# Unread float16 products on TensorE in the first eleven attention tiles

## The chip, the cores and the metric

The kernel runs on one core of one Trainium2 chip. The metric is the device time of one execution in microseconds (us); the time of a kernel is the median of its runs. The profile is of one execution. Engines are named as the profile names them: PE is TensorE (PEld its weight loads), DVE VectorE, ACT ScalarE, POOL GpSimd, SP the queue that issues most of the DMAs.

## The reference

Attention with rotary positions over 4 batches of 8 heads, 576 positions and 64 dimensions, then two feed-forward layers over the 2304 tokens of 512 numbers:

```python
q_rot, k_rot = (rotate(q), rotate(k))
scores = scale * np.matmul(q_rot, k_rot.transpose(0, 1, 3, 2))
scores = scores - np.max(scores, axis=-1, keepdims=True)
attn = np.exp(scores)
attn = attn / (np.sum(attn, axis=-1, keepdims=True) + 1e-09)
x = np.matmul(attn, v)                       # then (2304, 512)
h = np.maximum(np.maximum(x @ w1, x @ w2), x @ w3)
y = h @ w_out                                # moe_w_out, 768 wide inside
h = y @ w_in
out = (h * (1.0 / (1.0 + np.exp(-h)))) @ w_out   # moe2, 2048 wide inside
```

The weights arrive as float64 and are brought to pairs of float16 numbers (a high and a low part) inside the kernel.

## The kernel before

Attention goes by pairs of heads, (batch, pair), and within a pair by tiles of 128 query rows: tiles 0 and 1 of all four pairs of a batch first, then tiles 2, 3 and 4 (tile 4 holds the last 64 rows of both heads). In the order of the program the tiles of batch 0 are numbered here 0 to 19, so tiles 0 and 1 are those of the first pair, 2 and 3 of the second, 4 and 5 of the third, 6 and 7 of the fourth, and 8 to 10 the rest of the first pair.

A pair is loaded (`load_qk`), rotated on DVE or POOL (`qk_rope`, L330 to L334), and turned on PE (`qk_turn`: four transposes for k and four for q, L348, one more for the last 64 positions, L354), with copies out of PSUM on DVE and ACT (L350 to L360). A tile then goes through these steps: scores on PE (`tile_scores`, L387 and L390, or L380 and L381 for a tile of 64 rows), the negative row maximum on DVE (L400), the exponential on ACT for each head (`e`, L407), the division on ACT (L416, L419; reciprocal on DVE, L417), nine transposes on PE (`tile_turn`, L448) with copies on ACT (L452) and DVE (L454), and, once two or three tiles of a pair are turned, the product with v (`av`, L463 and L467). The scores have one buffer, `s`, of three banks: the next tile's scores wait until both exponentials have read the last ones.

Beside these tiles the weights of the first layer are prepared (`prep_w1`): twelve loads of 768 KB each into four staging places, each piece converted on ACT (L214, and L218 for the first) or POOL (L216), joined on DVE (L225, L226), measured on ACT (L140), and split on POOL (L160) and DVE (L163). A staging place is loaded anew once DVE's L226 has read it. From tile 8 on the first layer's products (`moe1`, written by `group`, L538, into the two banks `m` of the ring `ps_m`) are mixed into the tiles.

Each engine works off its instructions in the order of the program. That order is not the order in which the code is written: a scheduler with its own timing of the instructions interleaves the engines' work, and `tc.issue_after(x)` keeps an instruction behind x. So a change of one engine's work can change the order on all of them.

Of the kernel before, what the change touches and what calls it, by code (L numbers as in the profile page):

```python
# [7 lines left out]
F32 = mybir.dt.float32  # L8
F16 = mybir.dt.float16
# [8 lines left out]
P = 128  # L18
# [4 lines left out]
def fused_kernel(  # L23
# [22 lines left out]
    nc = tc.nc  # L46
# [28 lines left out]
    ps_m = Ring(ctx, "ps_m", 2, space=PSUM)  # L75
# [8 lines left out]
    ident = const.tile([P, P], F32, name="ident")  # L84
# [67 lines left out]
    def flat(t):  # L152
        return t.rearrange("p a b -> p (a b)")
# [95 lines left out]
    last = {}  # L249
# [59 lines left out]
    def qk_rope(b, hp):  # L309
        t = raw_t[b, hp]  # L310
        w = w_p.tile([P, 18, D], F32, tag="w", name="w")
        if b:
            with tc.issue_after(last["pool"]):
                return rope_steps(t, w, nc.gpsimd, ((0, 6), (6, 12), (12, 18)))
        if hp == 1:
            with tc.issue_after(last["kd"]):
                rope_steps(t, w, nc.vector, ((8, 16), (16, 18)))
            return rope_steps(t, w, nc.gpsimd, ((0, 4), (4, 8)))
        if hp == 0:
            return rope_steps(t, w, nc.vector, ((8, 16), (0, 8), (16, 18)))  # L320
        return rope_steps(t, w, nc.gpsimd, ((0, 6), (6, 12), (12, 18)))
# [15 lines left out]
    def qk_turn(b, hp):  # L337


        t = raw_t.pop((b, hp))  # L340
        T = t_p.tile([P, 576 + 512], F32, tag="T", name="T")
        K, Q = kd[(NP * b + hp) % NK], qd[(NP * b + hp) % NK]
        for i in (1, 0):
            tr = ps_t.tile([P, 512], F32, tag="tr", name="tr")
            for c in range(4):
                behind = tc.issue_after(last["s"]) if b == 0 and hp > 1 else nullcontext()
                with behind:
                    nc.tensor.transpose(tr[:, c * P:(c + 1) * P], flat(t[:, 8 * i + 2 * c:8 * i + 2 * c + 2, :]), ident)  # L348
            if i == 0:
                last["T"] = nc.scalar.activation(out=T[:, 0:512], in_=tr, func=AF.Copy, scale=0.125).ins  # L350
            else:
                nc.vector.tensor_copy(out=T[:, 512:1024], in_=tr)
        tr = ps_t.tile([P, 512], F32, tag="tr", name="tr")
        nc.tensor.transpose(tr[:, 0:P], flat(t[:, 16:18, :]), ident)  # L354
        nc.scalar.activation(out=T[:, 1024:1088], in_=tr[:, 64:128], func=AF.Copy)
        rs = (slice(0, 64), slice(64, 128))
        for r in rs:
            nc.scalar.activation(out=Q[r, r], in_=tr[r, 0:64], func=AF.Copy, scale=0.125)
        for r in rs:
            last["kd"] = nc.vector.tensor_copy(out=K[r, r], in_=tr[r, 64:128]).ins  # L360
        T_t[b, hp] = T, K, Q
# [8 lines left out]
    def both(s, o, step, n):  # L370

        return bass.AP(tensor=s.tensor, offset=s.offset + o, ap=[list(s.ap[0]), [step, 2], [1, n]])
    evacs = [0]

    def tile_scores(key):
        b, hp, t = key
        T, K, Q = T_t[b, hp]
        s = ps_s.tile([P, 1536], F32, tag="s", name="s")
        if t == 4:
            nc.tensor.matmul(s[:, 0:512], Q, T[:, 512:1024], start=True, stop=True)  # L380
            nc.tensor.matmul(s[:, 512:576], Q, T[:, 1024:1088], start=True, stop=True)  # L381
            s_t[key] = s
            return
        n = P
        qs = T[:, t * P:t * P + n]
        kt = T[:, 512:1024]
        nc.tensor.matmul(both(s, 512, 448, 64), qs, K, start=True, stop=True)  # L387
        for g, o in ((0, 0), (1, 1024)):
            r = slice(64 * g, 64 * g + 64)
            last["s"] = nc.tensor.matmul(s[:, o:o + 512], qs[r], kt[r], start=True, stop=True).ins  # L390
        s_t[key] = s

    def heads(key):
# [27 lines left out]
    def tile_turn(key):  # L421
        b, hp, t = key
        n = P
        e = e_t.pop(key)
        r = int(t > 1)
        q0, w = PARTS[r][:2]
        if (b, hp, r) not in pt_t:
            pt_t[b, hp, r] = pt_p.tile([P, 9, w], F32, tag="pt", name="pt")
        pt = pt_t[b, hp, r]
        o = P * t - q0  # L430
        if t == 4:
            tr = ps_t.tile([P, 512], F32, tag="tr", name="tr")
            for c in range(4):
                nc.tensor.transpose(tr[:, c * P:(c + 1) * P], e[:, c * P:(c + 1) * P], ident)
            t4 = tr.rearrange("p (c g q) -> p c g q", c=4, g=2)
            nc.scalar.activation(out=pt[:, 0:4, o:o + 64], in_=t4[:, :, 0], func=AF.Copy)
            nc.vector.tensor_copy(out=pt[:, 5:9, o:o + 64], in_=t4[:, :, 1])
            tr = ps_t.tile([P, 512], F32, tag="tr", name="tr")
            nc.tensor.transpose(tr[:, 0:P], e[:, 448:576], ident)
            nc.tensor.transpose(tr[0:64, P:2 * P], e[:, 512:576], ident)  # L440
            nc.scalar.activation(out=pt[0:64, 4, o:o + 64], in_=tr[0:64, P:P + 64], func=AF.Copy)
            nc.vector.tensor_copy(out=pt[64:128, 4, o:o + 64], in_=tr[64:128, 64:128])
            return
        for j in range(3):
            tr = ps_t.tile([P, 512], F32, tag="tr", name="tr")
            for i in range(3):
                c = 3 * j + i
                nc.tensor.transpose(tr[:, i * n:(i + 1) * n], e[0:n, c * P:(c + 1) * P], ident[0:n, 0:n])  # L448
            to, of = pt[:, 3 * j:3 * j + 3, o:o + n], tr[:, 0:3 * n].rearrange("p (a n) -> p a n", a=3)
            evacs[0] += 1  # L450
            if evacs[0] % 3 == 1 if evacs[0] < 28 else evacs[0] % 3:
                nc.scalar.activation(out=to, in_=of, func=AF.Copy)  # L452
            else:
                nc.vector.tensor_copy(out=to, in_=of)  # L454
# [28 lines left out]
    def at(j, f, *a):  # L483
        events.setdefault(j, []).append((f, a))
# [14 lines left out]
    for b in range(1, B):  # L499
# [3 lines left out]
            at(u - 2, v_max, b, hp)  # L503
        at(u, v_scale, b)

    def attention():

        for j in range(len(tiles) + 4):
            if j < len(tiles):
                tile_scores(tiles[j])  # L510
                tile_max(tiles[j])
            if 1 <= j <= len(tiles):
                tile_norm(tiles[j - 1])
            if 2 <= j <= len(tiles) + 1:
                tile_turn(tiles[j - 2])
            for f, a in events.pop(j, ()):
                f(*a)
            yield


# [616 lines left out]
    for hp in range(NP):  # L1137
        load_v(0, hp)
    last["max"] = qk_rope(*pairs[0]).ins
    qk_turn(*pairs[0])  # L1140
    wprep = prep_w1(stage1)
    for j in sorted(e for e in events if e < 0):
        for f, a in events.pop(j):
# [133 lines left out]
```

## Time and profile before

| | |
|---|---|
| median of 3 runs | 1037.62 us (1037.03 to 1039.41) |
| the profiled execution | 1035.59 us |
| its span, first to last instruction | 1033.9 us |
| granted clock of TensorE, mean over the span | 0.976 |
| busy: PE, PEld | 962.4 us (93%), 717.0 us (69%) |
| busy: DVE, ACT, POOL | 688.3, 616.3, 489.6 us (67%, 60%, 47%) |

Start times in the rows count from the first instruction of the span. A row gives the start, the time that the row covers (of several equal instructions from the start of the first to the end of the last), the engine, the line, the operation and how many. In brackets stands how long the engine was idle before it, and what ended that wait. [...]

### The profile page before, as it was taken

To read this page: it belongs to the slowest core of one execution; us is meant where nothing else is said; L and a number is where in the kernel's file an instruction comes from. 1 tells how busy PE (TensorE), PEld (TensorE's weight loads), DVE (VectorE), ACT (ScalarE), POOL (GpSimd) and SP (SyncE) were. 2 spreads that over 40 slices of the span, in tenths; PEclk is the share of its full clock that TensorE was granted. 3 is DMA by queue.
4 is the path that set the end of the run, shared out by engine and by line. 5 is a ranking of instruction groups with operands and counts; after the bars stand their busy time and mean duration, and the time that the engine had idled before them with its cause. 6 is when DMAs were issued, how large, how long until landed. Compare 5 with 4: busy or idle time off the path is not lost.

```text
span 1033.9 us, 19511 instructions
## 1 busy us (share of the span) xinstructions
PE 962.4 (93%) x7234; PEld 717.0 (69%) x7234; DVE 688.3 (67%) x1295; ACT 616.3 (60%) x1377; POOL 489.6 (47%) x548
## 2 busy tenths in 40 slices
PE   4677998999999999998999999999999999999997
PEld 2343664666666766655756668777888888888887
DVE  6769877765567655687566646645678767867454
ACT  3778676566666575867767754534455644644352
POOL 6735593961127720354223205536258457346164
PEclk9688999999999999999999999999999999999999
DMA  6943132422334510653444415254345244342201
GB/s 152 280 115 101 33 97 75 129 71 62 102 109 110 137 47 27 189 147 118 144 123 139 143 58 168 82 187 145 128 144 168 92 152 125 108 129 93 90 3 41
DMA packets 126062, 117.99 MB, mean 114 GB/s; under 512 B 47376, under 2 KB 109584, under 8 KB 125968
## 3 DMA queue, kind: packets, MB, share of 16 engines
q1 hardware_dynamic: 124464, 116.03, 37.4%
q8 instruction: 57, 0.93, 0.4%
q10 hardware_dynamic: 1504, 0.72, 0.3%
q14 instruction: 37, 0.30, 0.1%
HBM read 90.51 MB, written 26.21 MB: 113 GB/s over the span
## 4 chain that ended last, share of the span: by engine, by line
PE 62%; DVE 9%; ACT 6%; POOL 6%; DMA 6%; issue 3%; SPq 1%; ACTq 0%; DVEq 0%; POOLq 0%
PE m L538 18%; PE xp L467 6%; PE m L946 5%; PE s L390 5%; PE tr L448 5%; PE mb L946 4%; POOL gsum L893 4%; PE mg L538 3%; PE c L1010 3%; PE a L1010 2%; PE b L1010 2%; POOL yr L981 2%; DVE nb L400 1%; PE d L1010 1%; DVE g L898 1%
## 5 line engine op out<-in xcount | busy, mean ns | idle before, releaser
L538 PEld LDWEIGHTS <-w 128*128 128x128 f16 x1632 | 157.3, 98 | 68.8 <-issue 27.8
L538 PE MATMUL m<-x,w 128*128 128x256 f16 (+1 forms) x1336 | 189.7, 288 | 9.9 <-ACT t L554 4.0
L1010 PEld LDWEIGHTS <-g 128*128 128x128 f16 x1485 | 145.7, 98 | 19.9 <-issue 2.3
L946 PEld LDWEIGHTS <-w8s 128*128 128x128 f16 x1344 | 131.4, 98 | 20.3 <-issue 4.8
L400 DVE TENSOR_REDUCE nb<-s 128x2 f32<-128x1152 f32 (+1 forms) x80 | 98.7, 1234 | 49.4 <-PE s L390 39.5
L212 POOL TENSOR_SCALAR z<-z 128x256 uint16<-128x256 uint16 x64 | 56.0, 875 | 159.2 <-DVE z L211 148.4
L407 ACT ACTIVATE e<-s,nb 128x576 f32<-128x576 f32 x144 | 105.1, 735 | 29.0 <-DVE nb L400 24.9
L419 ACT ACTIVATE e<-e,rec 128x576 f32<-128x576 f32 x144 | 104.5, 768 | 17.8 <-DVE rec L417 17.5
L448 PE MATMUL tr<-ident,e 128*128 128x128 f32 x576 | 97.4, 289 | 14.2 <-ACT T L350 6.2
L787 POOL TENSOR_TENSOR z<-z 128x128 f32<-128x128 f32 (+1 forms) x96 | 59.0, 634 | 105.5 <-DMA z<-zwo 38.4
L448 PEld LDWEIGHTS tr<-ident,e 128*128 128x128 f32 x576 | 69.8, 147 | 50.0 <-issue 13.4
L946 PE MATMUL m<-yr,w8s 128*128 128x256 f16 x768 | 90.8, 273 | 3.7 <-DVE t L952 3.7
L452 ACT ACTIVATE pt<-tr 128x384 f32<-128x384 f32 x119 | 56.8, 486 | 47.9 <-PE tr L448 47.7
L467 PE MATMUL xp<-pt,vd 128*64 128x256 f32 (+1 forms) x512 | 84.6, 419 | 0.0
L390 PE MATMUL s<-T 64*128 64x512 f32 x256 | 83.7, 698 | 0.0
L960 POOL TENSOR_TENSOR z<-t 128x256 f32<-128x256 f32 x32 | 28.0, 875 | 95.8 <-DVE t L952 55.9
L946 PE MATMUL mb<-yr,w8s 128*128 128x256 f16 x576 | 69.9, 274 | 2.3 <-ACT yr L158 2.1
L538 PE MATMUL m<-h,wo 128*128 128x256 f16 (+1 forms) x448 | 64.9, 286 | 0.1
L898 DVE SCALAR_TENSOR_TENSOR g<-gsum,sg,g 128x1024 f16<-128x1024 f32 x36 | 49.1, 1373 | 22.1 <-ACT g L897 21.6
L538 PEld LDWEIGHTS <-wo 128*128 128x128 f16 x512 | 49.3, 98 | 16.9 <-issue 4.0
L897 ACT ACTIVATE g<-gsum,sg 128x1024 f16<-128x1024 f32 x36 | 40.7, 1140 | 32.8 <-POOL gsum L893 32.8
L330 POOL TENSOR_TENSOR w<-qk,sin_sb 128x384 f32<-128x384 f32 (+1 forms) x44 | 45.7, 1058 | 30.4 <-DMA qk<-in_q_dram 16.0
(231 smaller groups left out, 1910.8 us busy)
## 6 DMA issues: line engine op xcount, KB each, us to landing
w8s<-w8scr SPq DMA_DIRECT2D x64, 448.0 KB, 4.2
z<-in_moe_w_in_dram SPq DMA_DIRECT2D x32, 256.0 KB, 3.2
z<-in_moe_w_out_dram SPq DMA_DIRECT2D x32, 256.0 KB, 3.3
w<-in_moe_w_dram SPq DMA_DIRECT2D x6, 768.0 KB, 6.0
wo<-in_moe_w_dram SPq DMA_DIRECT2D x6, 768.0 KB, 4.6
qk<-in_q_dram SPq DMA_DIRECT2D x32, 128.0 KB, 3.0
vd<-in_v_dram SPq DMA_DIRECT2D x16, 256.0 KB, 3.0
zwi<-z SPq DMA_DIRECT2D x32, 128.0 KB, 3.1
```

The costliest lines, as they stand in the source:

```text
L390: last["s"] = nc.tensor.matmul(s[:, o:o + 512], qs[r], kt[r], start=True, stop=True).ins
L400: x = nc.vector.tensor_reduce(out=nb[:, 0:m], in_=both(s, 0, 960, 576) if m > 1 else s[:, 0:576], op=ALU.max, axis=AX.X, negate=True)
L407: x = nc.scalar.activation(out=e[:, HK[g]], in_=s[:, SK[g]], func=AF.Exp, bias=nb[:, g:g + 1], accum_out=sm[:, g:g + 1])
L419: nc.scalar.activation(out=e[:, HK[g]], in_=e[:, HK[g]], func=AF.Copy, scale=r[:, g:g + 1])
L448: nc.tensor.transpose(tr[:, i * n:(i + 1) * n], e[0:n, c * P:(c + 1) * P], ident[0:n, 0:n])
L452: nc.scalar.activation(out=to, in_=of, func=AF.Copy)
L467: nc.tensor.matmul(xp[r, 0:n], v4[:, g, c, :], pt[:, c + 5 * g, :], start=False, stop=(c == 3))
L538: nc.tensor.matmul(ps[:, 0:n], l, r, start=(first and i == 0), stop=(not more and i == len(passes) - 1))
L787: nc.gpsimd.tensor_tensor(out=z[:, o], in0=z[:, x], in1=z[:, y], op=op)
L898: nc.vector.scalar_tensor_tensor(out=l, in0=x, scalar=sg_t[jb], in1=h, op0=ALU.mult, op1=ALU.subtract)
L946: nc.tensor.matmul(o, l, r, start=(i == 0), stop=(i == len(passes) - 1))
L1010: x = nc.tensor.matmul(ps, l, r, start=first, stop=last_, skip_group_check=True)
```

## The change

PE gets 200 more products. Each multiplies the identity matrix, its float32 bytes read as float16, with itself: a weight load of 128x128 and a product of 128x256 float16 into a bank `m` that nobody reads. Fifty stand ahead of the first turn. Ten stand behind the first turn (`pe_q`). In each of the first eleven steps of the loop over tiles seven follow the scores of the step's tile (`pe_s`), and from the third step on seven more follow the turn of that step (`pe_t`), nine times. Nothing of the computation is removed. Since the line numbers shift, L448 of before is L449 of the changed kernel, L407 is L408, L400 is L401, L452 is L453; lines up to L354 stay, and the new product is L514.

```diff
-        nc.tensor.transpose(tr[:, 0:P], flat(t[:, 16:18, :]), ident)
+        last["pe_q"] = nc.tensor.transpose(tr[:, 0:P], flat(t[:, 16:18, :]), ident).ins
...
+        last["pe_s"] = last["s"]
...
-                nc.tensor.transpose(tr[:, i * n:(i + 1) * n], e[0:n, c * P:(c + 1) * P], ident[0:n, 0:n])
+                last["pe_t"] = nc.tensor.transpose(tr[:, i * n:(i + 1) * n], e[0:n, c * P:(c + 1) * P], ident[0:n, 0:n]).ins
...
+    idle = ident.bitcast(F16)
+
+    def warm(n, after=None):
+
+        ps = ps_m.tile([P, 512], F32, tag="m", name="m")
+        with tc.issue_after(after) if after else nullcontext():
+            for _ in range(n):
+                nc.tensor.matmul(ps[:, 0:256], idle[:, 0:P], idle, start=True, stop=True)
...
+            if j < 11:
+                warm(7, last["pe_s"])
+                if j > 1:
+                    warm(7, last["pe_t"])
             yield
...
     last["max"] = qk_rope(*pairs[0]).ins
+    warm(50)
     qk_turn(*pairs[0])
+    warm(10, last["pe_q"])
```

The order on PE at the start of the program, before: the turn of the first pair, the scores of tile 0, the turn of the second pair, the scores of tile 1.

```order
L348 MATMUL tr_222<-ident_78,qk_151 128x128 x4
L354 MATMUL tr_228<-ident_78,qk_151 128x128
L387 MATMUL s_299<-kd_0_122,T_215 128x2x64
L390 MATMUL s_299<-T_215 128x512 x2
L348 MATMUL tr_272<-ident_78,qk_160 128x128 x4
L348 MATMUL tr_266<-ident_78,qk_160 128x128 x4
L387 MATMUL s_316<-kd_0_122,T_215 128x2x64
```

The same place in the changed kernel, with one pair of weight load and product for each run of ten, or seven:

```order
L348 MATMUL tr_273<-ident_78,qk_151 128x128 x4
L354 MATMUL tr_279<-ident_78,qk_151 128x128
L514 LDWEIGHTS ident_78
L514 MATMUL m_286<-ident_78 128x256
...
L387 MATMUL s_361<-kd_0_122,T_266 128x2x64
L390 MATMUL s_361<-T_266 128x512 x2
L514 LDWEIGHTS ident_78
L514 MATMUL m_374<-ident_78 128x256
...
L348 MATMUL tr_334<-ident_78,qk_160 128x128 x4
L348 MATMUL tr_328<-ident_78,qk_160 128x128 x4
L354 MATMUL tr_340<-ident_78,qk_160 128x128
L387 MATMUL s_386<-kd_0_122,T_266 128x2x64
```

The ten stand between the first turn and the scores of tile 0, seven behind these scores; the second pair's last transpose (L354) now stands ahead of the scores of tile 1.

The order on ACT from the exponentials of tile 1 to the first of tile 2, before (`e_322` is tile 1, `e_343` tile 2; `w` and `wo` are staging and weights):

```order
L407 ACTIVATE e_322,sm_323<-s_316,nb_320 128x576 x2
L214 ACTIVATE w_0_138<-w_0_295 128x768
L416 ACTIVATE rec_347<-sm_323 128x2
L218 ACTIVATE w_0_295<-w_0_295 128x768
L419 ACTIVATE e_322<-e_322,rec_347 128x576 x2
L214 ACTIVATE w_0_138<-w_1_312 128x768
L140 ACTIVATE junk_394,w1m_136<-w_0_138 128x768
L214 ACTIVATE w_0_138<-wo_0_141 128x768
L350 ACTIVATE T_368<-tr_375 128x512
L407 ACTIVATE e_343,sm_344<-s_337,nb_341 128x576 x2
```

The same stretch of ACT in the changed kernel (`e_392` is tile 1, `e_421` tile 2, `e_496` tile 3):

```order
L408 ACTIVATE e_392,sm_393<-s_386,nb_390 128x576 x2
L417 ACTIVATE rec_425<-sm_393 128x2
L420 ACTIVATE e_392<-e_392,rec_425 128x576 x2
L350 ACTIVATE T_446<-tr_453 128x512
L408 ACTIVATE e_421,sm_422<-s_415,nb_419 128x576
L214 ACTIVATE w_0_138<-w_0_357 128x768
L408 ACTIVATE e_421,sm_422<-s_415,nb_419 128x576
```

The first weight piece (L214) moves from ahead of tile 1's division to between tile 2's two exponentials; L218, two more L214 and the measuring L140 move behind tile 2's exponentials, and stand ahead of those of tile 3.

The order on PE from the scores of tile 5 to those of tile 6, before (`tr_499` is the turn of q of the fourth pair):

```order
L387 MATMUL s_520<-kd_0_124,T_368 128x2x64
L390 MATMUL s_520<-T_368 128x512 x2
L448 MATMUL tr_474<-ident_78,e_343 128x128 x3
L448 MATMUL tr_540<-ident_78,e_402 128x128 x3
L348 MATMUL tr_499<-ident_78,qk_248 128x128 x4
L448 MATMUL tr_572<-ident_78,e_454 128x128 x3
L463 MATMUL xp_587<-pt_463,vd_0_127 128x256
L448 MATMUL tr_535<-ident_78,e_402 128x128 x3
L387 MATMUL s_556<-kd_0_125,T_492 128x2x64
```

The same stretch in the changed kernel (`tr_609` is the same turn of q):

```order
L387 MATMUL s_646<-kd_0_124,T_446 128x2x64
L390 MATMUL s_646<-T_446 128x512 x2
...
L348 MATMUL tr_609<-ident_78,qk_310 128x128 x4
...
L449 MATMUL tr_666<-ident_78,e_496 128x128 x3
L449 MATMUL tr_661<-ident_78,e_496 128x128 x3
L449 MATMUL tr_714<-ident_78,e_564 128x128 x3
L464 MATMUL xp_729<-pt_573,vd_0_127 128x256
L387 MATMUL s_698<-kd_0_125,T_602 128x2x64
```

That turn of q now follows tile 5's scores with only five of the new products between, where it stood behind two groups of transposes; the transposes of tile 2 (`e_343` before) have moved ahead of tile 5's scores. From PE's row 963 of 12062 on (the new products not counted) PE's order is the same as before; on DVE, ACT, POOL and SP the last difference stands likewise in the first fifth to third of their rows.

## Rows read from the trace of the kernel before

**Rows 1.** By stretch: length, busy PE, PEld, DVE, ACT, POOL, then clock, DMA share, GB/s.

```profile
0.00:110.00 110.00, 71.23 (x326) 39.94 (x327) 79.43 (x141) 74.00 (x163) 60.30 (x64) 0.83 0.54 153
80.00:100.00 20.00, 12.90 (x67) 6.66 (x65) 20.00 (x27) 16.03 (x36) 11.16 (x7) 0.91 0.42 131
110.00:1033.90 923.90, 891.14 (x6911) 677.06 (x6908) 608.88 (x1155) 542.34 (x1215) 429.31 (x485) 0.99 0.36 110
```

**Rows 2.** PE in order of time: the same work at either clock.

```profile
46.23 2.08 PE L390 MATMUL s<-T 64*128 64x512 f32 x4
...
52.51 1.13 PE L390 MATMUL s<-T 64*128 64x512 f32 x4
53.57 0.55 PE L448 MATMUL tr<-ident,e 128*128 128x128 f32 x3
...
60.33 1.11 PE L348 MATMUL tr<-ident,qk 128*128 128x128 f32 x4 [2.94 <-DVE pt L454]
61.24 0.85 PE L448 MATMUL tr<-ident,e 128*128 128x128 f32 x3
...
63.94 2.08 PE L390 MATMUL s<-T 64*128 64x512 f32 x4
65.95 0.88 PE L448 MATMUL tr<-ident,e 128*128 128x128 f32 x6
...
100.07 2.84 PE L538 MATMUL m<-x,w 128*128 128x256 f16 x12 [3.02 <-ACT t L554]
...
193.48 0.60 PE L348 MATMUL tr<-ident,qk 128*128 128x128 f32 x4
```

**Rows 3.** ACT in order of time: first exponentials of the tiles, and a weight piece.

```profile
19.13 0.74 ACT L407 ACTIVATE e<-s,nb 128x576 f32<-128x576 f32 x1 [0.41 <-DVE nb L400]
...
24.38 0.73 ACT L407 ACTIVATE e<-s,nb 128x576 f32<-128x576 f32 x1
...
28.88 0.92 ACT L214 ACTIVATE w<-w 128x768 f32<-128x768 f32 x1 [2.96 <-DMA w<-in_moe_w_dram]
...
35.68 0.73 ACT L407 ACTIVATE e<-s,nb 128x576 f32<-128x576 f32 x1
...
42.18 0.74 ACT L407 ACTIVATE e<-s,nb 128x576 f32<-128x576 f32 x1
...
58.21 0.74 ACT L407 ACTIVATE e<-s,nb 128x576 f32<-128x576 f32 x1 [1.00 <-DVE nb L400]
...
67.52 0.74 ACT L407 ACTIVATE e<-s,nb 128x576 f32<-128x576 f32 x1 [2.38 <-DVE nb L400]
...
75.52 0.73 ACT L407 ACTIVATE e<-s,nb 128x576 f32<-128x576 f32 x1
...
101.58 0.75 ACT L407 ACTIVATE e<-s,nb 128x576 f32<-128x576 f32 x1
```

**Rows 4.** The chain of work that ended last, two of its pieces.

```profile
69.72 4.59 DMA w<-in_moe_w_dram
...
137.36 2.73 PE m L538 x24
```

**Rows 5.** POOL in order of time: the identity, and weight pieces of the first loads.

```profile
1.61 0.29 POOL L264 TENSOR_SCALAR_AFFINE_SELECT ident<-ident 128x128 f32<-128x128 f32 x1
...
38.49 4.66 POOL L216 TENSOR_SCALAR wo<-wo 128x768 uint16<-128x768 uint16 x2
```

**Rows 6.** The first turn on PE, and DVE around it, in order of time.

```profile
9.95 1.09 PE L348 MATMUL tr<-ident,qk 128*128 128x128 f32 x4 [9.95 <-DVE qk L334]
...
10.69 0.69 DVE L334 TENSOR_TENSOR qk<-qk,w 128x512 f32<-128x512 f32 x1
...
13.66 0.46 DVE L360 COPY kd<-tr 64x64 f32<-64x64 f32 x2 [1.68 <-ACT qd L358]
...
17.74 1.36 DVE L400 TENSOR_REDUCE nb<-s 128x2 f32<-128x1152 f32 x1
```

More of the change, by code (lines that the diff above doesn't have):

```diff
@@ L380, in tile_scores @@
             nc.tensor.matmul(s[:, 0:512], Q, T[:, 512:1024], start=True, stop=True)
-            nc.tensor.matmul(s[:, 512:576], Q, T[:, 1024:1088], start=True, stop=True)
+            last["pe_s"] = nc.tensor.matmul(s[:, 512:576], Q, T[:, 1024:1088], start=True, stop=True).ins
             s_t[key] = s
@@ L439, in tile_turn @@
             nc.tensor.transpose(tr[:, 0:P], e[:, 448:576], ident)
-            nc.tensor.transpose(tr[0:64, P:2 * P], e[:, 512:576], ident)
+            last["pe_t"] = nc.tensor.transpose(tr[0:64, P:2 * P], e[:, 512:576], ident).ins
             nc.scalar.activation(out=pt[0:64, 4, o:o + 64], in_=tr[0:64, P:P + 64], func=AF.Copy)
```

## The prediction

> **What bounds the kernel now.** I read the page first, then the busy time by stretch, then PE, ACT and DVE in order of time up to 110 us, and last the chain of waits. The page says that PE is busy 93% of the span and that its clock is low only near the start. The stretches say where [rows 1]: from 110 us on PE works 891.1 of 923.9 us at a clock of 0.99, so that part is PE's and no product can be saved there. Up to 110 us PE works 71.2 us, DVE 79.4 and ACT 74.0, and none is full: there the time goes into a loop. Scores wait for the last exponential, the row maximum for the scores, the exponential for the maximum, and weight pieces stand between them on ACT and DVE. In this part the clock is 0.83 in the mean. What the low clock costs is seen on equal work [rows 2]: a tile's scores take 2.08 us against 1.13, three transposes 0.85 against 0.55, four transposes of a turn 1.11 against 0.60. The clock is low where PE had stood idle before, and comes back in a run without a break: after an idle 2.94 us PE works from 60.33 to 65.95, 5.62 us, at the low level, and the transposes from 65.95 on have the high one.
>
> So the change is worth what it brings forward the tiles by, up to about tile 11 (101.58 in rows 3); after that PE is the bound and its order is the old one, so a lead is kept.
>
> **The price of the new products.** They have the form of L538's, 128x256 float16 with a weight load each: 24 take 2.73 us on the chain, 0.114 us each [rows 4]; at the low clock 12 take 2.84, 0.237 each [rows 2]. The identity is ready at 1.61 + 0.29 = 1.90 us [rows 5]. Fifty from there end at 7.6 us if all have the high clock and at 13.8 if all have the low one. By the run above (5.62 us low, then high) I take 24 at the low clock and 26 at the high one: 1.90 + 5.62 + 2.96 = 10.5 us. The first turn started at 9.95, so it starts 0.5 late, but four transposes take 0.60 instead of 1.09. The other 150 cost 17.1 us at the high clock, 35.6 at the low. PE's idle time up to 110 us is 38.8, of which 9.95 lie before the first turn [rows 1, 6]; 28.8 are left, so 150 at the high clock fit beside idle time and 150 at the low one do not. I take nothing for them on the path: seven stand behind scores, while DVE and ACT work for some 3 us on that tile (L400's 1.36, two exponentials at 0.74), and seven behind a turn, whose copies are then due. Without that cover a run of seven costs 0.8 us, or 1.66 at the low clock. They wait for nothing but a bank `m`: where a scale's maximum (L120) used it, one run waits for DVE's reading, and behind it on PE stand only transposes whose divisions on ACT are later still.
>
> **The sum, by the lead at each tile.**
>
> Tile 0: the second turn needs DVE's L334, which ends at 10.69 + 0.69 = 11.38; turned at the high clock from there it ends at 12.0, half a microsecond earlier, and so do the copies to `kd` at 13.66 [rows 6]. The scores gain 0.95 more, but DVE has the second pair's rotation to finish before the row maximum at 17.74, so that is hidden. Lead 0.5.
>
> Tile 1: scores before had the low clock only in part; of 0.95 I take 0.5 (ends 0 and 0.95).
>
> Tiles 2 and 3: here it is the order. Before, ACT stood 2.96 us in front of the first weight piece until its load had landed at 28.88, with tile 1's division and a turn's copy queued behind it; the exponential of tile 2 came at 35.68, 11.3 us after tile 1's [rows 3]. Now these stand ahead of the piece, which meets its load between tile 2's exponentials. Tile 2 thus gains several microseconds, but L218, two L214 and L140 now stand in front of tile 3, and POOL's pieces for the first loads still run to 38.49 + 4.66 = 43.15 [rows 5]. So what is late next is tile 3's exponential. Of the 2.96 I keep 1.8 at tile 3 (ends 0 and 2.96).
>
> Tile 4: its scores had the low clock (2.08 at 46.23) and were followed directly by the maximum: 0.95.
>
> Tile 6: the run from 60.33 lies on the loop; the exponential of tile 6 waited for it, 9.31 us after that of tile 5 [rows 2, 3]. The kinds shown shrink from 1.11 + 0.85 + 2.08 = 4.04 to 2.28 us, a factor of 0.56; 5.62 us become 3.17, a gain of 2.45. The turn of q at its head, which had waited 2.94 for a copy of DVE, now stands right behind tile 5's scores: I take 1.0 of that (ends 0 and 2.94).
>
> Tiles 7 to 11: between 80 and 100 us DVE has no gap at all [rows 1], and tile 7 waits for a weight load of 4.59 us [rows 4] that DVE's L226 behind tile 6's maximum releases. These move with the lead but do not add to it. The twelve products at 100.07 (2.84, at the high clock 1.37) I count as hidden by DVE (ends 0 and 1.47).
>
> Sum: 0.5 + 0.5 + 1.8 + 0.95 + 2.45 + 1.0 = 7.2 us. The profiled execution took 1035.59, so 1028.4; it was 2.03 below the median of 1037.62, so the median becomes **1030.4**. What the changed order does between 110 and about 200 us I take as nothing, with 1.5 either way.
>
> [...]
>
> **Rivals.**
>
> The clock does not hold. Gaps stay in the loop (ACT and DVE are still shared with the weights), and if PE is low again by tile 3, the clock's own terms go (0.5 + 0.5 + 0.95 + 2.45 = 4.4), the 2.8 of the order remains, and seven products at the low clock on the path take 1.66 of it: a gain of 1.1 to 2.8, about 1035.6. For it: a single idle 2.94 us sufficed before 60.33. Against: the runs of seven stand just in such gaps. [...]
>
> The lead is lost to the weights. If DVE, full from 80 to 100 us, and the reloading of four staging places set the pace by themselves, the tiles come early and the first layer's products wait as before: 1037.6. For it: DVE's 20.0 of 20 us. Against: up to 80 us DVE has idle time, and its pieces there are released by the same tiles that come earlier.
>
> The new products get in the way, so that it is slower. On PE they stand in a fixed order ahead of what comes next: eleven in front of tile 5's scores, fourteen in front of a turn at tile 7. With 63 of the 150 on the path (63 x 0.114 = 7.2) the gain is gone; with 90 it is 3 us slower, 1040.6. Against: PE's 28.8 us of idle time.
>
> More than forecast: with the upper ends of tiles 1, 2, 6 and the late products the sum is 0.5 + 0.95 + 2.96 + 0.95 + 2.45 + 2.94 + 1.47 = 12.2, or 1025.4.
>
> **How the numbers follow.** A measurement of this kernel can tell about 0.2%, 2.1 us, from no change. Forecast, a gain of 4.4 to 10 us (1027.6 to 1033.2): 0.52. More than 10: 0.08. The clock does not hold: 0.18, half of it beyond 2.1 us. Lost to the weights: 0.12, a quarter of it beyond. In the way: 0.10. Faster 0.52 + 0.08 + 0.09 + 0.03 = 0.72; the same 0.18; slower 0.10. The range reaches from 1025, the sum of the upper ends, to 1038, which takes in both cases near no change and leaves out the slower one.
>
> **What would show it.** Right: the first turn within 1 us of 10.5 and at 0.60; no ACT wait of 3 us ahead of the first L214 with tile 1's division behind it; the first exponentials of tiles 3, 6 and 11 near 39.4, 60.3 and 94.4 (2.8, 7.2 and 7.2 ahead); nearly all scores at 1.13; PE's order and busy time after that as before. Wrong: a granted clock of 0.5 in 30 to 50 us; a first turn after 12 us; waits of PE on the weights (L160, L163) that grow by what the tiles gained; or scores that start later than the exponentials before them end, with new products in between.

## The result: slower, and the profile after

The changed kernel takes 1045.89 us (median of 7 runs, 1041.27 to 1048.43) against 1037.62 beside it (7 runs, 1035.11 to 1039.82). The ratio is 1.0074, with a 95% interval from 1.0047 to 1.0100: 8 us slower, where 7 us faster was forecast. The profiled execution took 1048.03 us, its span 1046.3.

Busy time by stretch after, the stretches of [rows 1] and two of 10 us:

```profile
core 0: us, PE busy (x) PEld busy (x) DVE busy (x) ACT busy (x) POOL busy (x), PEclk, DMA share, GB/s
0.00:110.00 110.00, 88.28 (x510) 55.67 (x510) 77.87 (x132) 71.49 (x156) 56.88 (x63) 0.89 0.55 153
80.00:100.00 20.00, 17.18 (x113) 10.81 (x113) 20.00 (x26) 13.04 (x30) 8.99 (x7) 1.00 0.36 106
110.00:1046.30 936.30, 897.78 (x6926) 680.92 (x6924) 614.29 (x1163) 545.64 (x1222) 429.75 (x485) 0.99 0.36 108
...
150.00:160.00 10.00, 6.26 (x48) 4.69 (x45) 9.96 (x18) 6.32 (x18) 9.76 (x10) 1.00 0.17 39
160.00:170.00 10.00, 7.42 (x32) 3.64 (x32) 5.16 (x11) 3.90 (x11) 8.33 (x9) 0.66 0.37 104
```

Up to 110 us the products are there (PE 88.28 us for 71.23) and the granted clock, a share of full speed, is higher (0.89 for 0.83). But the stretch behind 110 us, where nothing was added, takes 936.3 us instead of 923.9. And between 150 and 170 us PE is busy only 13.7 of 20 us, before 16.1:

```profile
150.00:160.00 10.00, 6.68 (x41) 4.82 (x38) 9.86 (x20) 6.91 (x22) 6.86 (x7) 0.90 0.51 138
160.00:170.00 10.00, 9.37 (x50) 4.58 (x49) 6.25 (x22) 5.45 (x16) 0.69 (x1) 0.93 0.19 49
```

Two cautions. The profiled executions lie 12.4 us apart, the medians 8.3: 4.7 us of the 12.4 fall between tiles 25 and 72, where the orders agree (last section). And up to 20 us the clock column reads 1.00 in the profile of before, though a turn takes 1.09 us and a tile's scores 2.08 there; for that stretch only the durations tell the clock.

The start went as worked out. PE in order of time:

```profile
1.96 8.02 PE L514 MATMUL m<-ident 128*128 128x256 f16 x50 [1.96 <-POOL ident L264]
10.11 0.66 PE L348 MATMUL tr<-ident,qk 128*128 128x128 f32 x4
11.64 0.66 PE L348 MATMUL tr<-ident,qk 128*128 128x128 f32 x4 [0.88 <-DVE qk L334]
```

The fifty end at 10.0 (forecast 10.5), and the first turn takes 0.66 us for 1.09 [rows 6]. Tile 0's row maximum still starts at 17.96, as before at 17.74: it stands on DVE behind the second pair's rotation. Its scores, 14.01 to 15.53, had long been there.

The first exponentials of tiles 3, 6 and 11 start at 42.35, 64.69 and 105.63 us: 0.2 later, 2.8 earlier and 4.1 later than in [rows 3]. The lead that was to be 7.2 at tile 11 is gone before the products end.

The largest stretch of idle time behind 110 us is near 160 us. POOL from W1's second scale (L160 with `sw11s`) to the end of the third rotation of the second batch (L330 to L334):

```profile
116.83 0.91 POOL L160 TENSOR_SCALAR w<-w,sw11s 128x768 f16<-128x768 f32 x1 [9.69 <-DVE sw11i L133]
...
128.94 1.61 POOL L216 TENSOR_SCALAR w<-w 128x512 uint16<-128x512 uint16 x1 [2.10 <-ACT wo L214]
...
134.49 3.82 POOL L330 TENSOR_TENSOR w<-qk,sin_sb 128x384 f32<-128x384 f32 x3
...
159.10 3.24 POOL L330 TENSOR_TENSOR w<-qk,sin_sb 128x384 f32<-128x384 f32 x3
...
165.42 2.92 POOL L334 TENSOR_TENSOR qk<-qk,w 128x384 f32<-128x384 f32 x3
```

Before, the scale was met 7.5 us sooner, and this rotation ended at 157.0 and not at 168.3:

```profile
109.37 0.90 POOL L160 TENSOR_SCALAR w<-w,sw11s 128x768 f16<-128x768 f32 x1 [5.50 <-DVE rec L417]
...
146.58 2.92 POOL L330 TENSOR_TENSOR w<-qk,sin_sb 128x384 f32<-128x384 f32 x3
...
155.01 2.01 POOL L334 TENSOR_TENSOR qk<-qk,w 128x384 f32<-128x384 f32 x2
```

DVE in the changed kernel beside the last of it, and PE (a product with v, av, is L468 here):

```profile
154.60 0.95 DVE L225 TENSOR_SCALAR wo<-wo 128x512 int32<-128x512 int32 x1
155.48 1.56 DVE L226 SCALAR_TENSOR_TENSOR wo<-w,wo 128x512 int32<-128x512 int32 x1
156.96 1.21 DVE L577 TENSOR_TENSOR h<-t,h 128x256 f16<-128x256 f32 x1
...
158.43 1.14 DVE L226 SCALAR_TENSOR_TENSOR wo<-w,wo 128x512 int32<-128x512 int32 x1
159.50 0.45 DVE L360 COPY kd<-tr 64x64 f32<-64x64 f32 x2
...
160.65 0.77 DVE L145 TENSOR_SCALAR wo1m<-wo1m 128x6 f32<-128x6 f32 x1
161.45 0.92 DVE L146 TENSOR_SCALAR wo1m<-wo1m 128x6 int32<-128x6 int32 x1
...
162.62 0.95 DVE L147 TENSOR_SCALAR wo1m<-wo1m 128x6 int32<-128x6 int32 x1
163.61 0.23 DVE L443 COPY pt<-tr 64x64 f32<-64x64 f32 x1
```

```profile
155.32 0.60 PE L348 MATMUL tr<-ident,qk 128*128 128x128 f32 x4
...
160.09 0.30 PE L440 MATMUL tr<-ident,e 128*128 128x128 f32 x1 [2.82 <-DVE kd L360]
...
163.89 0.90 PE L449 MATMUL tr<-ident,e 128*128 128x128 f32 x3 [2.20 <-DVE pt L443]
...
165.79 3.10 PE L468 MATMUL xp<-pt,vd 128*64 128x320 f32 x16
168.82 0.49 PE L387 MATMUL s<-kd,T 128*128 128x128 f32 x2
```

PE in the kernel before:

```profile
155.72 0.30 PE L439 MATMUL tr<-ident,e 128*128 128x128 f32 x1 [1.73 <-DVE kd L360]
...
158.11 1.54 PE L448 MATMUL tr<-ident,e 128*128 128x128 f32 x6 [1.08 <-ACT pt L452]
...
160.65 2.76 PE L467 MATMUL xp<-pt,vd 128*64 128x320 f32 x16
```

In the changed kernel PE waits 2.82 us for the two `kd` copies of a pair of the second batch, where it waited 1.73: DVE does these only behind three pieces of the narrowing (L225, L226, which join the parts of a weight piece) of the weights WO1 and a result (L577). Then it waits 2.20 us for L443, which stands behind L145 to L147; before, it waited at that place 1.08 for a copy of ACT. Both hold up the chain to tile 20's scores. No new product is near. The last seven end at 95.1; what is left of the change here is the order in which the scheduler put the queues, and how early or late the tiles arrive.

### The profile page after: what moved, and what is told of

It is laid out like the page before. It is cut to its first block, busy times and chain, and to the rows that moved or that the text cites. A ratio compares the mean times of both kernels' runs of the same rounds, so it can differ in the third digit from the quotient of the medians.

```text
span 1046.3 us, 19917 instructions
## 1 busy us (share of the span) xinstructions
PE 986.1 (94%) x7434; PEld 736.6 (70%) x7434; DVE 692.2 (66%) x1295; ACT 617.1 (59%) x1377; POOL 486.6 (47%) x548
## 4 chain that ended last, share of the span: by engine, by line
PE 60%; DVE 13%; POOL 6%; ACT 6%; DMA 5%; issue 4%; SPq 1%; ACTq 0%; DVEq 0%; POOLq 0%
PE m L552 17%; PE xp L468 6%; PE m L960 5%; PE s L390 5%; PE tr L449 4%; PE mb L960 4%; POOL gsum L907 4%; PE mg L552 3%; PE c L1024 3%; PE b L1024 2%; PE a L1024 2%; DVE nb L401 2%; POOL yr L995 1%; PE d L1024 1%; PE s L387 1%
## 5 line engine op out<-in xcount | busy, mean ns | idle before, releaser
L552 PEld LDWEIGHTS <-w 128*128 128x128 f16 x1632 | 159.6, 99 | 68.3 <-issue 29.9
L401 DVE TENSOR_REDUCE nb<-s 128x2 f32<-128x1152 f32 (+1 forms) x80 | 98.7, 1234 | 52.2 <-PE s L390 41.8
L408 ACT ACTIVATE e<-s,nb 128x576 f32<-128x576 f32 x144 | 105.2, 736 | 34.6 <-DVE nb L401 29.6
L420 ACT ACTIVATE e<-e,rec 128x576 f32<-128x576 f32 x144 | 104.6, 770 | 16.7 <-DVE rec L418 16.3
L449 PE MATMUL tr<-ident,e 128*128 128x128 f32 x576 | 95.9, 283 | 16.5 <-DVE pt L455 7.7
L449 PEld LDWEIGHTS tr<-ident,e 128*128 128x128 f32 x576 | 68.5, 144 | 47.7 <-issue 14.0
L468 PE MATMUL xp<-pt,vd 128*64 128x256 f32 (+1 forms) x512 | 88.3, 429 | 0.0
L453 ACT ACTIVATE pt<-tr 128x384 f32<-128x384 f32 x119 | 56.9, 487 | 50.8 <-PE tr L449 50.6
L390 PE MATMUL s<-T 64*128 64x512 f32 x256 | 78.9, 668 | 0.0
L468 PEld LDWEIGHTS xp<-pt,vd 128*64 128x64 f32 x512 | 37.5, 140 | 35.9 <-issue 19.3
L330 POOL TENSOR_TENSOR w<-qk,sin_sb 128x384 f32<-128x384 f32 (+1 forms) x44 | 45.2, 1049 | 29.8 <-DMA qk<-in_q_dram 19.7
```

Source lines behind the costliest of these rows:

```text
L401: x = nc.vector.tensor_reduce(out=nb[:, 0:m], in_=both(s, 0, 960, 576) if m > 1 else s[:, 0:576], op=ALU.max, axis=AX.X, negate=True)
L408: x = nc.scalar.activation(out=e[:, HK[g]], in_=s[:, SK[g]], func=AF.Exp, bias=nb[:, g:g + 1], accum_out=sm[:, g:g + 1])
L420: nc.scalar.activation(out=e[:, HK[g]], in_=e[:, HK[g]], func=AF.Copy, scale=r[:, g:g + 1])
L449: last["pe_t"] = nc.tensor.transpose(tr[:, i * n:(i + 1) * n], e[0:n, c * P:(c + 1) * P], ident[0:n, 0:n]).ins
L468: nc.tensor.matmul(xp[r, 0:n], v4[:, g, c, :], pt[:, c + 5 * g, :], start=False, stop=(c == 3))
L552: nc.tensor.matmul(ps[:, 0:n], l, r, start=(first and i == 0), stop=(not more and i == len(passes) - 1))
```

## The experiments

Three things can cost: the order, the 60 products in front, and the runs of seven. To part them, most kernels below hold the queues to a given order. After everything is recorded, each engine's instructions are chained by constraints that fix the order alone (the old order held so was not slower, see the control below):

```diff
+def hold(nc, tc):
+    by = {}
+    for i in nc.cur_bb.bb.instructions:
+        if i.name not in FILL:
+            by.setdefault(str(i.engine).split(".")[1], []).append(i)
+    for e, ks in ORDER.items():
+        for x, y in zip(ks, ks[1:]):
+            d = mybir.DependencyInfo(mybir.DependencyClass.NoSync, mybir.DependencyReason.DATA)
+            tc.add_manual_dep(by[e][y], by[e][x].name, d, reason="order")
...
         fused_kernel(tc, *args)
+        hold(nc, tc)
```

`ORDER` holds the places of one engine after the other, from the kernel before or the changed one, up to where the two orders agree for good; `FILL` has the products. In the rows of such kernels lines stand 90 to 100 higher (L360 is L451 to L458), the names are the same.

**The changed order without products**: the kernel before, `ORDER` of the changed one.

> This is the kernel before with none of the products; every engine is held to the order in which the changed kernel's scheduler put the first part of the program. Theory A (the order that the scheduler chose between 100 and 170 us costs the time): slower than before, 1043 to 1048 us, with tile 20's first exponential some 5 us late and the half-weight scale of W1 (L160 on POOL) first met near 116 us. Theory B (the products themselves cost it, by TensorE's time or by the bank that they hold): 1036 to 1039 us, as before. Theory C (the stretch from 100 to 170 us falls late by chance of the clock): 1037 to 1046 us, but with the loss somewhere else in the program.

Measured 1042.44 us, ratio 1.0045 (1.0023 to 1.0068). Tile 20's row maximum is 4.4 us later than before (3.1 later than in the control below), and the second scale is met at 114.66. About half of the loss is there with no product in the program; the median lies just under theory A's range.

**The products in the order of before**: the changed kernel with `ORDER` of before and `if j < 9`: nine tiles have their runs, not eleven.

> The fifty, the ten and the runs of seven behind the scores and turns of the first nine tiles (not eleven), with every engine held to the order that it had before the change. Theory A (order): no loss, 1030 to 1038 us; 1030 if the lead of the first tiles is kept, 1038 if it is given back by tile 8 as in the changed kernel. Theory B (the products): 1043 to 1047 us.

Measured 1043.71 us, 1.0041 (1.0018 to 1.0064). So the products cost in the old order too, within theory B's range: neither theory alone holds.

**The front alone and the runs alone, scheduler free**: `warm(7, ...)` taken out, or `warm(50)` and `warm(10, ...)`.

> The fifty and the ten alone, no runs behind scores and turns; the scheduler is free, and what it builds is within 135 of 12,062 TensorE rows of the changed kernel's order, and the same on POOL. Theory A (order): slower, 1042 to 1047 us. Theory B (products): the 60 end before tile 0, so 1034 to 1038 us.

> The runs of seven behind scores and turns alone, without the fifty and the ten; the scheduler is free and its order differs from both others (1246 TensorE rows stand elsewhere than before, 670 elsewhere than in the changed kernel). Theory A (order): no figure follows from the products, 1036 to 1047 us, and the time goes with when POOL meets the second scale of W1 and when it is through with the third rope. Theory B (products): 1043 to 1047 us.

Measured 1038.8 us, 1.0001 (0.9977 to 1.0026), and 1045.64 us, 1.0059 (1.0037 to 1.0082). The first contradicts theory A as it was put: nearly the changed late order, yet no loss. Its trace shows a reason: it arrives at tile 11 with 3.8 us of lead on the kernel before and loses 2.7 of them by tile 25.

**Front and runs, in either order**: the same omissions with `ORDER` of before (runs for nine tiles) and of the changed kernel.

> The fifty and the ten alone, every engine held to the order of before. Theory A alone (order costs, products are free): 1035 to 1038 us. Theory D (order and runs each cost some 4 to 5 us, and add up; the 60 in front cost nothing since PE is idle there until 10 us): 1034 to 1038 us, some 5 us under the kernel with the runs as well (1043.7). Theory E (it is the 60 in front that cost, by the phase in which they leave the clock): 1042 to 1045 us.

> The fifty and the ten alone, every engine held to the changed kernel's order. Theory A alone: 1044 to 1047 us, as the changed kernel. Theory D: the order's 4 us, less what the front brings: 1039 to 1043 us. Theory E: 1044 to 1048 us.

> The runs of seven behind scores and turns of the first nine tiles, without the 60 in front, every engine held to the order of before. Theory A alone: 1036 to 1039 us. Theory D: 1041 to 1045 us. Theory E: 1036 to 1039 us.

> The runs of seven behind scores and turns of all eleven tiles, without the 60 in front, every engine held to the changed kernel's order. Theory A alone: 1042 to 1045 us, as that order without products (1042.4). Theory D: 1046 to 1049 us. Theory E: 1042 to 1044 us.

Measured 1040.43 us, 1.0016 (0.9997 to 1.0036); 1047.83 us, 1.0081 (1.0052 to 1.0110); 1040.54 us, 1.0024 (1.0010 to 1.0039); 1042.21 us, 1.0042 (1.0024 to 1.0061). No theory holds for all four: E meets two (the changed order), A one, D none. The changed order is the dearer one in both pairs, 1.0081 against 1.0016 and 1.0042 against 1.0024, the second by about as much as the control below is off. The runs seem to cost in the order of before (1.0024) and not in the changed one (1.0042 beside 1.0045 without); for the front, whose six runs in the changed order lie from 1042.18 to 1051.78, it is not settled.

**Which part of the order**: the order of one kernel up to tile 10's row maximum (near 92 us), that of the other behind it. `ORDER` is composed of the two; the products are none, none, all, and the front.

> No products. Up to tile 10's row maximum (near 92 us) every engine is held to the changed kernel's order, from there on to the order of before. Theory F (the order costs its 4 to 5 us between 100 and 170 us, where POOL takes a narrowing ahead of the second scale's splits and turns the second batch late): no loss, 1034 to 1038 us. Theory G (the order costs in the first 92 us): 1042 to 1044 us, as that order throughout (1042.4).

> No products. The converse: the order of before up to tile 10's row maximum, the changed kernel's order behind it. Theory F: 1041 to 1045 us. Theory G: 1036 to 1039 us.

> The changed kernel with all its products and its own order up to tile 10's row maximum; behind it every engine is held to the order of before. Theory F: the 4 to 5 us of the order come back, 1040 to 1042 us, and what is left above 1038 is the products' (2 to 4 us). Theory G: 1045 to 1047 us, as the changed kernel.

> The fifty and the ten alone, with the order that the scheduler built for them (the front-only kernel) up to tile 10's row maximum, behind it that of before. Theory F: the front-only kernel measured 1038.8 with the bad late order, and led by 3 us at tile 13, so 1033 to 1036 us, which would be below before. Theory G: 1037 to 1040 us.

Measured 1041.07 us, 1.0021 (0.9998 to 1.0044); 1044.22 us, 1.0047 (1.0026 to 1.0068); 1042.15 us, 1.0029 (1.0006 to 1.0053); 1036.68 us, 0.9986 (0.9964 to 1.0008). Theory F meets its range in the second and misses the others, the third by 0.15 us; G meets none. With the late part alone the loss is there (1.0047, 4.9 us), and giving the changed kernel the old late order takes it from 1.0074 to 1.0029, some 4.5 us. The two other pairs that differ in the late order give less: 2.5 us without products (1.0045 against 1.0021), 1.6 for the front (1.0001 against 0.9986). The early part may cost too; its interval reaches no loss.

**Which piece of the late order**: in the changed order, DVE's two `kd` copies are moved ahead of two L226 (not of the L225 in front), and L443 ahead of L145. Shown is DVE's order with the moves:

```diff
 L225 TENSOR_SCALAR wo<-wo
+L360 COPY kd<-tr x2
 L226 SCALAR_TENSOR_TENSOR wo<-w,wo
 L577 TENSOR_TENSOR h<-t,h
 L570 SCALAR_TENSOR_TENSOR t<-m,t
 L226 SCALAR_TENSOR_TENSOR wo<-w,wo
-L360 COPY kd<-tr x2
 L570 SCALAR_TENSOR_TENSOR t<-m,t
 L438 COPY pt<-tr
+L443 COPY pt<-tr
 L145 TENSOR_SCALAR wo1m<-wo1m
 L146 TENSOR_SCALAR wo1m<-wo1m
 L577 TENSOR_TENSOR h<-t,h
 L147 TENSOR_SCALAR wo1m<-wo1m
-L443 COPY pt<-tr
```

> No products; the changed kernel's order on every engine with two moves on DVE alone, near 155 us: the two kd copies (L360) ahead of WO1's narrowing, and the copy of the last transposed tile (L443) ahead of L145. Theory H (the late order costs because these copies stand behind narrowing and mask work that runs slowly beside POOL's third rotation, PE waits 2.7 and 2.2 us for them, and the av behind them runs at the low clock): PE's two waits shrink to under 1 us, 1037 to 1040 us. Theory I (it is POOL's late rotation itself, or TensorE's order): 1041 to 1044 us, as that order without the moves (1042.4).

> The changed kernel with all its products and its own order, but for the same two moves on DVE. Theory H: the late 3 to 5 us come back, 1040 to 1043 us. Theory I: 1045 to 1047 us, as the changed kernel.

> The fifty and the ten alone in the order that the scheduler built for them, with the same two moves on DVE. Theory H: the front-only kernel measured 1038.8 and lost 8.7 us of its lead at these waits, of which some 3 come back: 1033 to 1036 us, below before. Theory I: 1037 to 1040 us.

Measured 1047.06 us, 1.0083 (1.0066 to 1.0100); 1044.59 us, 1.0061 (1.0040 to 1.0081); 1037.37 us, 0.9986 (0.9973 to 0.9999). All three lie above theory H's range, by 7.1, 1.6 and 1.4 us. PE in the first of these:

```profile
157.87 0.30 PE L537 MATMUL tr<-ident,e 128*128 128x128 f32 x1 [0.36 <-DVE kd L458]
...
161.85 1.72 PE L546 MATMUL tr<-ident,e 128*128 128x128 f32 x6 [3.56 <-DVE pt L535]
```

Without the moves, in that order, PE waited 2.62 us for the `kd` copies and 2.20 for L443. Now it waits 0.36 for the first, and 3.56 at the next copy (L438, here L535), which still stands behind the narrowing. The stretch from tile 11 to tile 25 shrinks in all three, by 2.4 and 1.0 us (table below) and, for the front alone, from 106.15 to 104.61. The medians do not show it. In two kernels they fall by less than the intervals tell apart (1.0074 to 1.0061, 1.0001 to 0.9986), and in the first they rise (1.0045 to 1.0083): its six runs lie from 1043.17 to 1048.31 though its program was changed only there. That is not explained. Its profile loses the time ahead of the change: tile 11's row maximum is at 102.34 against 99.93 without the moves, in the same order up to there.

**POOL earlier**: the changed order, no products; DVE's splits (L163) ahead of the narrowing between them, POOL's L216 behind the sixth L160.

> No products; the changed kernel's order, but DVE's five later splits of W1's second half (L163) are moved ahead of the WO1 narrowing between them, and POOL's narrowing (L216) behind the sixth of its own splits, so that POOL's rotation of the second batch starts some 5 us sooner; the kd copies stay where they are. Theory H: little, 1040 to 1043 us. Theory I, POOL late: the waits before tile 20 go, 1037 to 1040 us.

Measured 1043.26 us, 1.0045 (1.0028 to 1.0063). The edit missed its aim. POOL's six splits took 12.3 us for 17.7, but the narrowing put behind them and the next one, which waited 1.87 us for ACT, used most of that up, and the scale was met 1.9 us later: the third rotation ended at 166.21, without the edit at 166.12. Counted from tile 11 it ended 1.9 us sooner, and the stretch from tile 11 to 25 is no shorter for it (108.33 for 108.39). That is too little to tell whether POOL's lateness costs.

**Control and converse**: the kernel before held to its own order; and the same with the `kd` copies put behind tile 19's row maximum and two pieces of narrowing, and L443 behind a third.

> The kernel before with no products, every engine held to its own order by the same chain of order constraints that the other experiments use. It says how much two profiles of one order differ, above all whether the low-clock stretches of the first 110 us and the one near 475 us, which the profile of before lacks, are of the order or of the single execution. Every theory: 1036 to 1040 us, as before.

> The converse of the moves on DVE: no products, the order of before, but the two kd copies (L360) near 155 us stand behind three pieces of WO1's narrowing and the copy L443 behind the fourth. Theory H: PE waits for them some 2 us longer, 1039 to 1042 us. Theory I (the copies' place is nothing; POOL and TensorE's order make the loss): 1036 to 1039 us.

Measured 1036.28 us, 0.9983 (0.9968 to 0.9997), and 1040.42 us, 1.0024 (1.0009 to 1.0039). The control is the old order instruction for instruction, so a deviation of 0.17% says nothing here, and the two kernels at 0.9986 are not shown to beat before. The converse lies 4.1 us above the control. PE in the control, then in the converse:

```profile
157.09 0.30 PE L537 MATMUL tr<-ident,e 128*128 128x128 f32 x1 [1.58 <-DVE kd L458]
...
162.02 2.70 PE L565 MATMUL xp<-pt,vd 128*64 128x320 f32 x16
164.65 0.49 PE L485 MATMUL s<-kd,T 128*128 128x128 f32 x2
```

```profile
159.48 0.45 PE L537 MATMUL tr<-ident,e 128*128 128x128 f32 x1 [4.43 <-DVE kd L458]
...
164.02 3.11 PE L565 MATMUL xp<-pt,vd 128*64 128x320 f32 x16
167.06 0.49 PE L485 MATMUL s<-kd,T 128*128 128x128 f32 x2
```

Three copies moved on DVE make tile 20's scores 2.4 us later, and 0.4 of it is that the av behind the longer wait is slower. So theory H names something that costs in the old order: 2.8 us from tile 11 to 25 in the profiles, about half of the late loss. That it makes up half of the loss in the changed order is not shown, since there the moves back did not lower the median.

The profiles together, one execution each. Start of the row maximum (L400, L401 after) of some tiles in us, and the time between two of them:

| kernel | tile 4 | tile 6 | tile 11 | 6 to 8 | 11 to 25 |
|---|---|---|---|---|---|
| before | 48.39 | 66.07 | 99.07 | 13.70 | 103.50 |
| before, own order held | 48.76 | 67.46 | 100.40 | 13.63 | 103.48 |
| order of before, front | 47.27 | 65.31 | 98.31 | 13.69 | 105.53 |
| order of before, runs | 45.68 | 64.45 | 100.30 | 16.32 | 104.65 |
| order of before, front and runs | 45.92 | 63.54 | 99.23 | 16.16 | 105.62 |
| order of before, copies late | 48.59 | 67.14 | 100.08 | 13.63 | 106.24 |
| late order of before, all products | 52.58 | 63.35 | 101.15 | 16.51 | 104.19 |
| late order of before, no products | 50.09 | 62.32 | 104.00 | 20.21 | 104.65 |
| changed order, no products | 50.38 | 62.45 | 99.93 | 15.98 | 108.39 |
| changed order, front | 48.29 | 60.45 | 97.80 | 15.87 | 108.51 |
| changed order, runs | 47.67 | 58.61 | 96.65 | 16.55 | 108.70 |
| changed kernel | 52.54 | 63.20 | 101.10 | 16.40 | 108.29 |
| changed order late only, no products | 47.28 | 65.29 | 98.69 | 13.61 | 108.80 |
| changed order, copies first | 51.58 | 63.45 | 102.34 | 17.42 | 105.99 |
| changed kernel, copies first | 51.00 | 61.78 | 99.81 | 16.55 | 107.31 |
| changed order, POOL earlier | 51.08 | 63.04 | 101.89 | 17.29 | 108.33 |
| front alone, scheduler free | 46.04 | 59.20 | 95.31 | 13.50 | 106.15 |
| front alone, late order of before | 46.23 | 60.08 | 96.62 | 12.89 | 103.63 |

For tiles 4 to 8 only rows of one order compare, since the orders put other work between them. That the column from 11 to 25 may be compared is seen where the old order stands in front: 103.48 with the old one behind it, 108.80 with the changed one. There the old order takes 103.5 to 105.6 (106.24 with the copies late), the changed one, with its copies where they were, 108.3 to 108.8, with products or without: 2.7 to 5.3 us more. Of the 5.3, 3.9 are idle time of PE (13.1 against 9.1 us in the control), and 2.7 of these lie from 50 to 80 us behind tile 11's maximum, near 160 us; the rest goes with a lower clock (0.94 for 0.97). Not all of it hangs on the copies: from tile 20 to 25 the changed order takes 38.9 to 39.0 us and the old one 37.6 to 37.7, wherever the copies stand.

The early part of the changed order varies by itself. Its four profiles without products reach tile 11 at 99.93, 101.89, 102.34 and 104.00 us, four of the old early order at 98.69 to 100.40. That is 2.5 us later in the mean, with 4 us between executions of one and the same order; the 104.00 is from the slowest of its twelve runs.

In the order of before, too, a kernel with products loses behind tile 11, 1.3 to 1.5 us by tile 13. Tile 12's scores there, in the control and then with the products:

```profile
105.01 1.13 PE L488 MATMUL s<-T 64*128 64x512 f32 x4
```

```profile
104.07 2.08 PE L482 MATMUL s<-T 64*128 64x512 f32 x4
```

The clock in the 6 us behind tile 11's maximum was 0.72 in the control and 0.50 to 0.52 in the three profiles with front, runs or both. Whether the products bring this about or the single execution is not shown.

From tile 6 to 8, in the order of before, it is 13.6 to 13.7 us without runs and 16.2 to 16.3 with them. In the changed order it is 15.9 to 20.2 without and 16.4 to 16.6 with them, so there the runs cost nothing that shows. The windows from 60 to 80 us of the control, then of the products in the order of before:

```profile
60.00:80.00 20.00, 17.51 (x92) 10.86 (x94) 13.37 (x29) 14.38 (x33) 5.68 (x4) 0.82 0.40 109
```

```profile
60.00:80.00 20.00, 20.00 (x132) 13.34 (x131) 10.96 (x28) 13.88 (x29) 4.74 (x3) 0.95 0.40 109
```

and PE in the second, between the scores of tiles 6 and 7 (L606 are the products):

```profile
63.42 0.94 PE L606 MATMUL m<-ident 128*128 128x256 f16 x7
64.20 0.82 PE L541 MATMUL tr<-ident,e 128*128 128x128 f32 x6
64.85 0.93 PE L606 MATMUL m<-ident 128*128 128x256 f16 x7
65.71 1.08 PE L560 MATMUL xp<-pt,vd 128*64 128x256 f32 x6
66.72 0.94 PE L606 MATMUL m<-ident 128*128 128x256 f16 x7
67.49 0.82 PE L541 MATMUL tr<-ident,e 128*128 128x128 f32 x6
```

PE has not one gap in the 20 us with the products. Each run puts off what follows it by about 0.8 us.

## Why the prediction was wrong

**"What the changed order does between 110 and about 200 us I take as nothing, with 1.5 either way."** This step failed, and it is the largest single term. The order there costs some 4.5 us of the 8 (1.0074 against 1.0029), 4.1 on the row maxima from 11 to 25 of the same two kernels (108.29 against 104.19). I had seen that the queues differ and priced the difference at nothing because PE's own order is nearly the old one there. DVE's order is a part of it, where copies that PE waits for came behind narrowing: moved so in the old order, three copies cost 4.1 us against the control. Which instructions make up the rest stays open.

**"I take nothing for them on the path."** Failed for tiles 6 to 8. The 28.8 us of idle time on which I set the products are a sum over 100 us. In the profile of before 19.2 of them lie ahead of 60 us, 8.6 behind 80, and between, where tiles 6 to 8 and their avs run, 1.0. The control has PE busy there 17.5 of 20 us at a clock of 0.82, and at 0.95 the old work and the runs together fill it to 20.0. I named the price of the uncovered run, 0.8 us, rightly, and put the cover where there was none, in the old order. This is the rival "in the way", to which I gave 0.10.

**The clock's terms.** With the products the clock was higher: up to 110 us the profiles show 0.88 with front and runs in the order of before and 0.89 with the runs alone, for 0.81 in the control. In that order the sizes held too: at tile 4 the products lead by 2.8 to 3.1 us against the control (45.68 and 45.92 for 48.76), at tile 6 by 3.0 to 3.9, where I had 1.95 and 4.4 from the clock (against the profile of before, which runs ahead of the control there, only 1.6 to 2.5 at tile 6). But "a lead is kept" failed: the stretch from 6 to 8, where the runs stand, takes 2.5 to 2.7 of it back, and at tile 11 it is 0.1 to 1.2.

**Tiles 2 and 3, the order on ACT.** Mis-sized: tile 2's exponential came 4.0 us earlier (31.69), tile 3's 0.2 later for a term of +1.8. The weight pieces in front of it, four L214 between 32.41 and 42.33 with L218 and L140 among them, took all of the term: the lower end that I had named.

**Tile 0, "Lead 0.5."** It got nothing: the row maximum stands behind the rotation on DVE, which I had used as cover for the scores and not for the turn.

**The rivals.** "The clock does not hold" is not what happened: up to 110 us it was granted at 0.89 for 0.83, with the time slower. "Lost to the weights" named an engine that mattered, DVE, but not its order at 155 us. Its own place is not excluded: DVE is full from 80 to 100 us in both profiles, and tiles 8 to 11 take 21.5 us in the changed kernel for 19.3 before; no run here parts DVE's load from its order there.

What stays open: 3 us of the 8 remain with the old late order (1.0029), of which the early order without products has 1.0021 with an interval down to no loss. Why the moves of the copies do not lower the median in the changed order, and whether POOL's late rotation costs, stays open too. Why the front alone is dear in the changed order (1.0081) and free in its own (1.0001) isn't settled.

## What to carry to other kernels

Work that nobody reads still goes through the scheduler, and the order that it leaves behind, 60 us after its last instruction, can cost as much as the work; so compare the order of every engine, not only that of the one changed, and ask of each copy that moved who waits for it. Idle time is cover only where it lies: take the busy share of the stretch in which the new instructions stand, at the clock that they are to bring about, not the sum over the stage. To tell an order from the work, hold the old order and put the work in, and hold the new order and leave it out; and hold the old order alone as well, since that control lay 0.17% off here.

## What the runs showed of the hardware

Some of DVE's pieces took longer while POOL worked. In the profiles of before and of the changed kernel L226 took 0.68 and 0.69 us for 128x512 in the two cases in which POOL was idle, and 1.01 to 1.56 in the ten in which it worked for some or all of that time; L145 to L147 took 0.17 us for 128x6 in thirteen cases with POOL idle and 0.77 to 1.16 in five beside it. Not every piece was longer: L226 on 128x768 took 0.95 us at 50.72 in the profile of before, with POOL at work all the while, and 0.94 at 60.66, with POOL idle. The control's DVE, at a time when POOL stands idle (from 158.4 to 169.6):

```profile
158.77 0.68 DVE L324 SCALAR_TENSOR_TENSOR wo<-w,wo 128x512 int32<-128x512 int32 x1
...
162.19 0.17 DVE L243 TENSOR_SCALAR wo1m<-wo1m 128x6 f32<-128x6 f32 x1 [0.43 <-ACT junk L238]
```

These are L226 and L145. In the rows of the changed kernel above, where POOL works, L226 takes 1.56 and 1.14 us for 0.68, and L145 to L147 take 0.77 to 0.95 for 0.17. The copy L443 takes 0.23 in both; the two copies L360 take 0.45 in those rows, and 0.44 at 44.15 in the profile of before, where POOL is idle. Why some pieces take longer no run here shows. I had not weighed the longer pieces when I priced the order at nothing.

The transposes took less time where the granted clock was higher: of those in [rows 2], the three at 61.24 (0.85 us) stand where it was 0.51 (60 to 66 us), the six at 65.95 (0.88) where it was 1.00 (66 to 70 us). The first turn took 0.66 us right behind the fifty, 1.09 in [rows 6].

A part that no order touches varies too: from tile 25 to tile 72 the profiles of one and the same queue order take 359.3 to 364.8 us. From 460 to 490 us alone PE's idle time ranges from 1.5 to 5.0 us. So a difference of 5 us between two single profiles says nothing there.
